# Choosing which waiting step an engine's queue takes next: a priority order in place of first ready, first served

## The chip, the cores and the metric

The kernel runs on one core of one Trainium2 chip. The metric is the device time of one execution in microseconds (us); less is better. Engines are called as in the profile: PE (TensorE, with PEld for its weight loads), DVE (VectorE), ACT (ScalarE), POOL (GpSimd) and SP (SyncE, which issues DMAs).

## What is computed

Three layers stand one behind the other:

```python
# 1. attention: 4 batches, 8 heads, 576 tokens, head size 64, window 128, ALiBi bias
scores = scale * q @ k.T + bias          # masked to 0 <= i-j < 128
x = softmax(scores) @ v                  # -> 2304 tokens x 512
# 2. dense feed-forward, 512 -> 2048 -> 512
g = softplus(x @ w_in); x = g @ w_out
# 3. noisy top-2 of 8 experts, 512 -> 1024 -> 512
noisy = x @ w_gate + softplus(x @ w_noise) * noise
out[t] = sum over the two best e of  softmax_e * relu(x[t] @ w1[e]) @ w2[e]
```

Layer 2's weights come as 64-bit floats, the rest as 32-bit. The kernel splits every matmul operand into a high and a low part and adds three products (high x high, high x low, low x high).

## The kernel before, in words

**The work.** The 2304 tokens are 9 chunks of 256. Layer 2 has 16 feed-forward blocks of 128; each needs a weight of `w_in` and one of `w_out`, so there are 32 weights, numbered w0 to w31 (even: `w_in`). A job is one block of one chunk: `mm1` (L542) multiplies up into a PSUM tile `h` and starts a softplus on ACT, DVE and POOL (L565 to L574); `mm2` (L583) multiplies down into `y` or `z` three jobs later. The jobs go first over blocks 0 to 5 of all chunks (54 jobs), while the attention of later chunks is woven in, then over blocks 6 to 15 chunk by chunk. Jobs 0 to 2 are blocks 0 to 2 of chunk 0; from job 3 on, chunk 1 and the rest of chunk 0 alternate, until block 5 of chunk 0 is job 9.

**Attention** goes by pieces: `step_a` (L327) has PE write scores, DVE add the bias with the row minimum (L350), ACT take exponentials (L356), DVE the reciprocal of the sums (L361, L362), and POOL (L370) or ACT (L368) normalise; `step_b` (L377) has PE transpose and DVE or ACT copy (L399, L397); `step_c` (L404) has PE multiply with `v`, then ACT and DVE evacuate the high and low part (L429, L434).

**Weight conversion** (`w_convert`, L476): SP loads 512 KB of raw doubles; ACT L486 and L490; DVE L494, L495 and L496, which are one step; POOL L512; ACT L500; DVE L504 (for every third weight from w12 on POOL); for some weights SP stores the result. Five are under way at once; the first 12 are due at the start, then one more every two jobs. **Weight splits** (`w2_split`, L1128) are layer 3's counterpart: ACT L1141 takes the high part of a loaded weight, DVE L1139 the low part.

**Expert phase.** Routing (L689 to L775) writes a table of tokens per expert; `late_table` (L951) plans groups of 256 tokens. `g_rows` (L1024) loads a group's rows by DMA and merges them on DVE (L1036, L1037); POOL gathers tokens (L1048); `s1`, `s2`, `s3` (L1175 to L1260) are the matmuls, with relu in L1187 and L1188 and results added to `out` by POOL (L1249).

**What sets the order.** PE's order is written out by hand. Every other engine gets its instructions in the order in which a planner, class `Order` (L26), lets them out while the program is built. A chain (L38) is a list of steps, each with an engine and an estimated cost (`ca`, `cv`, `cv2`, `cg`, L96 to L109). A heap holds each chain's next step at the time when it is ready. `_pop` (L48) takes the earliest step. Before, a step whose engine is busy is let out all the same and booked behind the engine's last one:

```python
if eng is not None:
    when = max(when, self.free.get(eng, 0.0))
```

So each queue is first ready, first served, with the older chain first only in a tie. `need` (L75) pops until a key is there, and moves PE's clock; `emitted` (L70) pops without moving it. On the chip an engine runs its queue in that order, whatever is ready.

Of the kernel before, what the change touches and what calls it, by code (L numbers as in the profile page):

```python
# [25 lines left out]
class Order:  # L26
# [8 lines left out]
        self.free = {}  # L35
        self.parked = {}

    def chain(self, *steps, after=0.0):  # L38

        heapq.heappush(self.heap, (self.now + after, self.count, steps, 0))  # L40
        self.count += 1

    def done(self, key, when):
# [2 lines left out]
            heapq.heappush(self.heap, (max(when, entry[0]),) + entry[1:])  # L46

    def _pop(self):  # L48
        entry = when, count, steps, i = heapq.heappop(self.heap)
        eng, cost, fn, key, needs = (tuple(steps[i]) + (None,) * 5)[:5]  # L50
        for n in needs or ():
            if n not in self.fin:
                self.parked.setdefault(n, []).append(entry)
                return
            if self.fin[n] > when:
                heapq.heappush(self.heap, (self.fin[n], count, steps, i))
                return
        if eng is not None:
            when = max(when, self.free.get(eng, 0.0))
        end = when + cost  # L60
        if eng is not None:
            self.free[eng] = end
        if fn is not None:
            fn()
        if key is not None:
            self.done(key, end)
        if i + 1 < len(steps):
            heapq.heappush(self.heap, (end + (0.1 if eng is not None else 0.0), count, steps, i + 1))

    def emitted(self, key):  # L70
        while key not in self.fin:
# [24 lines left out]
def ca(n):  # L96
    return 0.16 + n * 0.00083


def cv(n):  # L100
    return 0.15 + n * 0.00104
# [6 lines left out]
def cg(n):  # L108
    return 0.05 + n * 0.00275  # L109
# [3 lines left out]
def moe_chain_kernel(ctx, tc, qk, v, w_in, w_out, w_gate, w_noise, noise, w1, w2, out):  # L113
    nc = tc.nc
    PE, ACT, DVE, POOL, SP = nc.tensor, nc.scalar, nc.vector, nc.gpsimd, nc.sync
# [26 lines left out]

    o_ = Order()
    chain, spend, need, emitted, mark = o_.chain, o_.spend, o_.need, o_.emitted, o_.mark
    NDMA = 16

# [11 lines left out]
    def f32(ap):  # L158
        return ap.bitcast(F32)
# [3 lines left out]
    def tl(pool, shape, dtype, name, bufs, fin, tag=None, slots=None):  # L163

        r = rings.setdefault(name, [])
        while len(r) >= bufs:
            last = r[-bufs]
            (need if pool is psum else emitted)(last)
            if r[-bufs] == last:
                break  # L170
        r.append(fin)
        return pool.tile(shape, dtype, name=name, tag=tag or name, bufs=slots or bufs)
# [126 lines left out]
    def dma(fn, key=None, nbytes=1 << 18, after=0.0, needs=()):  # L299
        chain(("SP", 0.06, fn, None, needs), ("DMA", nbytes / 330e3, None), (None, 2.0, None, key), after=after)  # L300
# [26 lines left out]
    def step_a(m0):  # L327
# [16 lines left out]
        for x in range(2):  # L344
            s = tl(att, [P, 512], F32, "s", NS, ("be", m0 + x))
            s = s.rearrange("p (h t) -> p h t", h=2)
            M[m0 + x] = dict(s=s)
            for j in range(2):
                def tail(s=s, x=x, j=j):
                    DVE.tensor_tensor_reduce(s[:nq, j, :n], ps[j][:nq, x, :n],  # L350
                                             relh[:nq, 2 * (m0 % 4 + x) + j, r0:r0 + n],
                                             -(D ** -0.5), 3.0e38, OP.add, OP.min, st[:nq, 0, 2 * x + j:2 * x + j + 1])

                def ex(s=s, x=x, j=j):
                    y = slice(2 * x + j, 2 * x + j + 1)
                    ACT.activation(s[:nq, j, :n], s[:nq, j, :n], AF.Exp, bias=st[:nq, 0, y], scale=-1.0,  # L356
                                   accum_out=st[:nq, 1, y])
                chain(("V", cv(n), tail, ("ttr", m0 + x, j)), ("A", ca(n) + 0.2, ex, ("ex", m0 + x, j)))
# [112 lines left out]
    def w_tile():  # L471
        return wpool.tile([P, 2, 512], F32R, name="w", bufs=NRING)
# [3 lines left out]
    def w_convert(i):  # L476
        fc, half = divmod(i, 2)
        d = {}

        def load():  # L480
            raw = d["raw"] = wpool.tile([P, 512, 2], I32, name="raw", tag="w", bufs=NRING)
            SP.dma_start(raw.rearrange("p n z -> p (n z)"), (w_out if half else w_in).bitcast(I32)[fc])

        def first():
            d["a"] = tl(mid, [P, 512], I32, "cva", 4, ("wl", i))
            ACT.activation(f32(d["a"]), f32(d["raw"][:, :, 1]), AF.Abs)  # L486

        def third():
            lo32 = d["raw"][:, :, 0]
            ACT.activation(lo32, lo32.bitcast(U32), AF.Copy, scale=2.0 ** -29)  # L490

        def bits():
            a = d["a"]
            DVE.tensor_scalar(f32(a), f32(a), F64_LO, F64_HI, op0=OP.max, op1=OP.min)  # L494
            DVE.tensor_scalar(a, a, 3, 0x3FFFFFFF, op0=OP.logical_shift_left, op1=OP.bitwise_and)  # L495
            DVE.scalar_tensor_tensor(a, d["raw"][:, :, 1], -0x40000000, a, op0=OP.bitwise_and, op1=OP.bitwise_or)  # L496

        def high():
            W[i] = w_tile()
            ACT.activation(W[i][:, 0], f32(d["a"]), AF.Copy)  # L500

        def low():
            t = W[i]
            (DVE if (i < 2 * NA or LOWV[i % len(LOWV)]) else POOL).tensor_tensor(t[:, 1], f32(d["a"]), f32(t[:, 0]), OP.subtract)  # L504

        def store():
            if i in sidx:
                SP.dma_start(scratch[sidx.index(i)], f32(W.pop(i)).rearrange("p z n -> p (z n)"))
                nfreed[0] += 1
        chain(("SP", 0.06, load), ("DMA", (1 << 19) / 330e3, None), (None, 2.0, None),  # L510
              ("A", ca(512), first), ("A", ca(512), third), ("V", 2.2, bits),
              ("P", cg(512), lambda: POOL.tensor_tensor(d["a"], d["a"], d["raw"][:, :, 0], OP.add), ("wa", i)),  # L512
              ("A", ca(512), high),
              ("V", cv(512), low, ("wl", i)) if (i < 2 * NA or LOWV[i % len(LOWV)]) else ("P", cg(512), low, ("wl", i)),
              (None, 0.0, lambda: mark_now(("w", i), ("wl", i))),
              ("SP", 0.06, store, ("st", i)))

    def mark_now(key, of):
        o_.done(key, o_.fin[of])
# [279 lines left out]
    def convert_some():  # L799

        while nconv[0] < due[0] and live1() < room() and (nconv[0] < NCV or ("w", nconv[0] - NCV) in o_.fin):
            w_convert(nconv[0])
            nconv[0] += 1
# [281 lines left out]
    def ring_left():  # L1085
        return NRING - live1() - inring[0] - 2 * nsplit[0]
# [37 lines left out]
    def skip_singles():  # L1124
        while wsp[0] < wl[0] and groups[WJ[wsp[0]][0]][0] == 1:
            wsp[0] += 1

    def w2_split():  # L1128
        skip_singles()
        j = wsp[0]  # L1130
        if j >= wl[0] or not splitting[0] or nsplit[0] >= NSPLIT or nback[0] < len(sidx) or ring_left() < 2:
            return False
        wsp[0] += 1
        nsplit[0] += 1
        t = RAW2[j]
        hi, lo = W2[j] = [wpool.tile([P, 1024], F32R, name=x, tag="w", bufs=NRING) for x in ("whi", "wlo")]

        def low():
            DVE.tensor_sub(lo, t, f32(hi))  # L1139
            w2_drop(j)  # L1140
        chain(("A", ca(1024), lambda: ACT.activation(hi, t, AF.Copy), None, (("r2", j),)),  # L1141
              ("V", cv(1024), low, ("w2", j)))
        return True

    def w2_drop(j):
        del RAW2[j]
        if j in extra:
            extra.remove(j)
        else:
            inring[0] -= 1  # L1150

    def pump():
        while w2_load():
            pass
        while w2_split():
            while w2_load():
                pass
# [170 lines left out]
    for t in range(NT + max(L2, len(items) + 2)):  # L1328
# [11 lines left out]
        if t in starts:  # L1340
            c, n = starts[t]
# [110 lines left out]
```

## Time and profile before

| | |
|---|---|
| three runs, median (lowest to highest) | 1137.41 us (1136.45 to 1138.78) |
| the profiled execution's own time | 1136.42 us |
| its span, first to last instruction | 1134.2 us |
| PE busy in the span | 1071.8 us (94%) |
| DVE / ACT / POOL busy | 748.8 / 616.2 / 509.9 us (66 / 54 / 45%) |
| mean granted TensorE clock | 0.978 |

The busy shares are means over stages with different limits, so they are to be read stage by stage: where PE is idle or at a lower clock, and what ended its waits.

### The profile page before, as it was taken

Reading aid. Unit: us, or ns where it says so; the run is one execution under the profiler, and the core shown is the slowest. Engines: PE = TensorE matmul, PEld = TensorE weight load, DVE = VectorE, ACT = ScalarE, POOL = GpSimd, SP = SyncE. Lnnn points to the kernel's source line nnn. Section 1 sums busy time; section 2 is a strip of 40 time slices with the busy share of each in tenths; the row PEclk is TensorE's granted clock in tenths of the full one; section 3 lists DMA queues with packets and bytes.
Section 4 is the critical chain, followed back from the end, with each engine's and each line's share of the span. In section 5 each row is a group of like instructions: output and inputs, shape, how many; then the busy total and the mean of one; then the engine's idle time right before and its main releaser. Section 6 shows DMA issues by size and latency. Waiting matters only on the chain.

```text
span 1134.2 us, 20933 instructions
## 1 busy us (share of the span) xinstructions
PE 1071.8 (94%) x7021; PEld 914.2 (81%) x7021; DVE 748.8 (66%) x1946; ACT 616.2 (54%) x1459; POOL 509.9 (45%) x535
## 2 busy tenths in 40 slices
PE   5589999999999999999998997999999999999997
PEld 3477777777789888888887886997997997999984
DVE  8975799988885677777767685653653653655520
ACT  7876778877764444444444543553553553555531
POOL 3455677766675566666674232222122223222112
PEclk8699999999999999999999998999999999999999
DMA  8231544554683322112348829788887888888722
GB/s 306 102 94 57 181 161 141 202 206 146 199 318 121 121 76 75 52 62 76 96 153 304 251 28 339 206 233 263 227 233 259 232 227 254 250 225 233 215 56 38
DMA packets 96557, 198.90 MB, mean 175 GB/s; under 512 B 34049, under 2 KB 44801, under 8 KB 96449
## 3 DMA queue, kind: packets, MB, share of 16 engines
q1 hardware_dynamic: 86112, 176.01, 47.2%
q0 software_dynamic: 10336, 21.54, 9.6%
q8 instruction: 56, 0.92, 0.3%
q14 instruction: 53, 0.43, 0.1%
HBM read 157.82 MB, written 39.69 MB: 174 GB/s over the span
## 4 chain that ended last, share of the span: by engine, by line
PE 76%; DVE 11%; DMA 5%; ACT 3%; issue 2%; POOL 1%; SPq 1%; POOLq 0%; DVEq 0%; ACTq 0%
PE h L190 35%; PE y L190 24%; PE z L190 10%; PE t L201 4%; PE t L190 3%; PE t L339 2%; DMA raw<-in_moe_w_out 1%; DVE s L350 1%; ACT s L356 1%; DVE w L504 1%; DVE cva L495 1%; DMA rawp<-in_moe_w 1%; DVE cva L496 1%; DVE cva L494 1%; DVE su L573 1%
## 5 line engine op out<-in xcount | busy, mean ns | idle before, releaser
L190 PE MATMUL h<-xh,w 128*128 128x256 f32 x1152 | 238.8, 290 | 4.3 <-DVE sl L568 4.2
L1139 DVE TENSOR_TENSOR wlo<-rawp,whi 128x1024 fp32r<-128x1024 f32 x107 | 130.7, 1222 | 133.8 <-ACT whi L1141 127.4
L1249 POOL DMA_INDIRECT out<-ys,rc x41 | 83.3, 2031 | 272.3 <-DVE ys L1258 131.9
L190 PEld LDWEIGHTS h<-xh,w 128*128 128x128 f32 x1152 | 190.7, 193 | 18.2 <-DVE sl L568 9.3
L1141 ACT ACTIVATE whi<-rawp 128x1024 fp32r<-128x1024 f32 x107 | 113.4, 1060 | 149.1 <-PE h L190 98.0
L190 PE MATMUL y<-w,gh 128*128 128x512 f32 x552 | 179.3, 406 | 0.1
L190 PE MATMUL h<-xh,whi 128*128 128x256 f32 x576 | 165.5, 287 | 6.5 <-DVE gl L1188 6.5
L190 PE MATMUL h<-xl,w 128*128 128x256 f32 x576 | 164.2, 285 | 3.1 <-DVE xl L434 3.1
L574 POOL TENSOR_TENSOR su<-sa,su 128x256 f32<-128x256 f32 x144 | 112.6, 782 | 113.1 <-DVE su L573 98.3
L190 PE MATMUL h<-xl,whi 128*128 128x256 f32 x576 | 163.3, 284 | 0.0
L190 PE MATMUL h<-xh,wlo 128*128 128x256 f32 x576 | 163.3, 283 | 0.0
L565 ACT ACTIVATE sa<-h 128x256 f32<-128x256 f32 x144 | 54.8, 381 | 157.5 <-PE h L190 116.0
L190 PEld LDWEIGHTS h<-xh,whi 128*128 128x128 f32 x576 | 110.1, 191 | 14.1 <-DVE gl L1188 6.9
L569 POOL TENSOR_TENSOR sl<-sl,su 128x256 f32<-128x256 f32 x144 | 109.7, 762 | 17.3 <-DVE sl L568 5.8
L190 PEld LDWEIGHTS h<-xl,w 128*128 128x128 f32 x576 | 111.1, 193 | 6.4 <-DVE xl L434 3.5
L190 PEld LDWEIGHTS h<-xl,whi 128*128 128x128 f32 x576 | 110.2, 191 | 7.1 <-issue 1.4
L190 PEld LDWEIGHTS h<-xh,wlo 128*128 128x128 f32 x576 | 110.2, 191 | 0.0
L190 PEld LDWEIGHTS y<-w,gh 128*128 128x128 f32 x552 | 95.0, 191 | 16.9 <-issue 3.2
L190 PE MATMUL y<-w,gl 128*128 128x512 f32 x276 | 108.6, 393 | 0.0
L1048 POOL DMA_INDIRECT xg<-x1buf,rc x41 | 42.4, 1035 | 105.6 <-DVE rc L1037 60.4
L572 DVE TENSOR_TENSOR gl<-sl,gh 128x256 fp32r<-128x256 f32 x144 | 81.0, 563 | 9.4 <-ACT gh L570 6.6
L370 POOL TENSOR_TENSOR s<-s,st 128x512 f32<-128x512 f32 (+2 forms) x72 | 72.2, 1011 | 33.2 <-DVE st L362 19.4
(256 smaller groups left out, 2281.5 us busy)
## 6 DMA issues: line engine op xcount, KB each, us to landing
rawp<-in_moe_w SPq DMA_DIRECT2D x140, 512.0 KB
raw<-in_moe_w SPq DMA_DIRECT2D x44, 512.0 KB
qkT<-in_qk SPq DMA_DIRECT2D x20, 512.0 KB
raw<-in_moe_w_in SPq DMA_DIRECT2D x16, 512.0 KB
raw<-in_moe_w_out SPq DMA_DIRECT2D x16, 512.0 KB
out<-zero SPq DMA_DIRECT2D x19, 256.0 KB
xspill<-xh SPq DMA_DIRECT2D x9, 512.0 KB
xspill<-xl SPq DMA_DIRECT2D x9, 512.0 KB
```

Source lines behind the costliest of these rows:

```text
L190: PE.matmul(o, l, r, start=start, stop=stop)
L201: PE.transpose(o, i, idn)
L339: PE.matmul(ps[j][:nq, x, :n].rearrange("p (s t) -> p s t", t=P), qkT[hd, u % NQK, 0, hp, :nq], qkT[hd, sl, 1, hp, :], start=True, stop=True)
L370: POOL.tensor_tensor(s[:nq, :, :n], s[:nq, :, :n], st[:nq, 3, 2 * x:2 * x + 2, None].to_broadcast([nq, 2, n]), OP.mult)
L565: chain(("A", ca(CT), lambda: ACT.activation(a, ph, AF.Abs)), ("A", ca(CT), lambda: ACT.activation(a, a, AF.Exp, scale=-1.0), ("e", t)), ( ...
L569: ("P", cg(CT), lambda: POOL.tensor_add(l, l, u), None, (("d", t),)),
L572: ("V", cv(CT), lambda: DVE.tensor_sub(gl, l, f32(gh)), ("g", t)))
L574: ("P", cg(CT), lambda: POOL.tensor_tensor(u, a, u, OP.subtract), ("d", t)), after=2 * ca(CT) + 0.15)
L1048: POOL.indirect_dma_start(out=x, out_offset=None, in_=x1buf[:T - 3 * CT if g < NEARLY else TPAD, :], in_offset=bass.IndirectOffsetOnAxis(a ...
L1139: DVE.tensor_sub(lo, t, f32(hi))
L1141: chain(("A", ca(1024), lambda: ACT.activation(hi, t, AF.Copy), None, (("r2", j),)), ("V", cv(1024), low, ("w2", j)))
L1249: POOL.indirect_dma_start(out=out[:, :], out_offset=bass.IndirectOffsetOnAxis(ap=rc[:, a, 0:1], axis=0), in_=ys, in_offset=None, compute_o ...
```

## The change

A heap entry gets a rank, `later`, between its time and its chain's number. A step whose engine is busy is no longer booked: it goes back into the heap at the time when the engine comes free, and all the steps that wait there are compared by rank, then by age of chain. Weight conversions and weight splits get rank 1, all other chains 0.

```diff
-    def chain(self, *steps, after=0.0):
+    def chain(self, *steps, after=0.0, later=0):
-        heapq.heappush(self.heap, (self.now + after, self.count, steps, 0))
+        heapq.heappush(self.heap, (self.now + after, later, self.count, steps, 0))
...
-        entry = when, count, steps, i = heapq.heappop(self.heap)
+        entry = when, later, count, steps, i = heapq.heappop(self.heap)
...
-                heapq.heappush(self.heap, (self.fin[n], count, steps, i))
+                heapq.heappush(self.heap, (self.fin[n], later, count, steps, i))
                 return
-        if eng is not None:
-            when = max(when, self.free.get(eng, 0.0))
+        if eng is not None and self.free.get(eng, 0.0) > when:
+            heapq.heappush(self.heap, (self.free[eng], later, count, steps, i))
+            return
...
-            heapq.heappush(self.heap, (end + (0.1 if eng is not None else 0.0), count, steps, i + 1))
+            heapq.heappush(self.heap, (end + (0.1 if eng is not None else 0.0), later, count, steps, i + 1))
...  (w_convert)
-              ("SP", 0.06, store, ("st", i)))
+              ("SP", 0.06, store, ("st", i)), later=1)
...  (w2_split)
-              ("V", cv(1024), low, ("w2", j)))
+              ("V", cv(1024), low, ("w2", j)), later=1)
```

No instruction is added or taken away, no cost estimate changes, and PE's own order stays as it is written.

## Rows read from the trace of the kernel before

**Rows 1.** Busy time by stage: window, length, engines, PE clock, DMA share, GB/s.

```profile
18.00:45.00 27.00, 14.90 (x83) 11.10 (x83) 26.41 (x55) 21.28 (x56) 13.16 (x10) 0.62 0.29 114
45.00:72.00 27.00, 19.05 (x151) 14.28 (x152) 25.65 (x75) 22.79 (x66) 14.98 (x13) 0.87 0.34 116
72.00:116.00 44.00, 42.16 (x331) 34.25 (x330) 25.15 (x103) 28.59 (x99) 24.52 (x31) 1.00 0.27 82
116.00:350.00 234.00, 224.33 (x1658) 181.45 (x1657) 200.68 (x551) 172.78 (x519) 161.16 (x177) 0.99 0.57 196
350.00:600.00 250.00, 248.44 (x1639) 218.15 (x1637) 178.61 (x573) 115.57 (x298) 151.50 (x197) 1.00 0.28 90
600.00:700.00 100.00, 87.67 (x561) 78.14 (x560) 68.03 (x201) 43.38 (x79) 35.18 (x30) 0.96 0.71 229
```

**Rows 2.** Waits of PE, 0 to 75 us: us in total, times, longest.

```profile
PE y L201 <- POOL s L370: 12.1, 3, 5.8
PE t L201 <- POOL s L370: 6.1, 3, 3.4
```

**Rows 3.** Groups of DVE, 0 to 72 us, the conversions: busy us, mean ns.

```profile
L504 DVE TENSOR_TENSOR w<-cva,w 128x512 fp32r<-128x512 f32 x12 | 9.4, 789 | 0.0
L494 DVE TENSOR_SCALAR cva<-cva 128x512 f32<-128x512 f32 x12 | 8.7, 727 | 0.0
L496 DVE SCALAR_TENSOR_TENSOR cva<-raw,cva 128x512 int32<-128x512 int32 x12 | 8.3, 693 | 0.4
...
L495 DVE TENSOR_SCALAR cva<-cva 128x512 int32<-128x512 int32 x12 | 7.6, 630 | 0.4
```

**Rows 4.** Timelines of PE and DVE, 23 to 34 us: start, length.

```profile
23.86 2.08 PE L339 MATMUL h<-qkT 64*128 64x256 f32 x8
...
31.79 2.39 PE L339 MATMUL h<-qkT 64*128 64x256 f32 x8 [3.27 <-DVE st L350]
...
27.91 1.52 DVE L494 TENSOR_SCALAR cva<-cva 128x512 f32<-128x512 f32 x1
...
30.53 0.42 DVE L350 CUSTOM_DVE_ANT_0 s<-h,relh 128x256 f32<-128x256 f32 x1
```

**Rows 5.** Timelines of ACT, DVE and PE, 33 to 40 us.

```profile
33.41 0.18 ACT L356 ACTIVATION_READ_ACCUMULATOR s<-s,st 128x1 f32 x1
...
37.98 0.16 DVE L361 TENSOR_SCALAR st<-st 128x4 f32<-128x4 f32 x1
...
39.62 1.12 PE L201 MATMUL y<-ident,s 128*128 128x128 f32 x4 [4.39 <-POOL s L370]
```

**Rows 6.** Timelines of ACT and DVE, 594 to 600 us: weight splits.

```profile
594.61 3.89 ACT L1141 ACTIVATE whi<-raw 128x1024 fp32r<-128x1024 f32 x4
...
596.26 3.49 DVE L1139 TENSOR_TENSOR wlo<-raw,whi 128x1024 fp32r<-128x1024 f32 x3
```

**Rows 7.** Timeline of PE, 603 to 699 us: the waits.

```profile
603.60 0.39 PE L190 MATMUL h<-xh,w 128*128 128x256 f32 x1 [3.27 <-DVE sl L568]
...
652.63 0.18 PE L190 MATMUL t<-mcum,ones 128*128 128x8 bf16 x1 [1.97 <-DVE mcum L757]
...
698.75 0.58 PE L190 MATMUL h<-xh,whi 128*128 128x256 f32 x1 [6.49 <-DVE gl L1188]
```

**Rows 8.** Groups of ACT and POOL, 0 to 72 us, the conversions: busy us, mean ns.

```profile
L490 ACT ACTIVATE raw<-raw 128x512 int32<-128x512 uint32 x12 | 8.0, 665 | 0.0
L486 ACT ACTIVATE cva<-raw 128x512 f32<-128x512 f32 x12 | 7.9, 658 | 0.6 <-DVE w L504 0.6
...
L500 ACT ACTIVATE w<-cva 128x512 fp32r<-128x512 f32 x12 | 7.5, 622 | 0.7 <-POOL cva L512 0.7
...
L512 POOL TENSOR_TENSOR cva<-cva,raw 128x512 int32<-128x512 int32 x12 | 16.7, 1390 | 26.0 <-DVE cva L496 16.6 <-DVE su L573 2.2 <-ACT pT L397 1.6
```

**Rows 9.** Timeline of DVE before the last of these waits.

```profile
696.42 0.17 DVE L1036 TENSOR_REDUCE rc<-rk 128x2 int32<-128x8 int32 x1 [9.23 <-DMA rk<-rect]
```

**Rows 10.** Instructions of L494, 0 to 72 us: ns min/median/max, starts.

```profile
L494 DVE TENSOR_SCALAR cva<-cva x12: 396/422/1524, 14.6 to 59.3; 128x512 f32<-128x512 f32 x12
```

## The prediction, made before the changed kernel ran

> **What bounds the kernel now.** I read the stages first, since only a stage in which PE idles has anything for a new order to give [rows 1]. From 350 to 600 us PE is busy 248.4 of 250 us. Before that it idles: 12.1 us of the 27 from 18 to 45, 8.0 of the 27 from 45 to 72, 1.8 of the 44 from 72 to 116, 9.7 of the 234 from 116 to 350; and after it 12.3 of the 100 from 600 to 700. In the first two of these DVE is busy 26.4 and 25.7 of 27 us: DVE is the bound there. PE's waits come next. Most of the start's idle time is waits for normalised scores from POOL, 12.1 and 6.1 us [rows 2]; POOL itself is busy only half the time, so what is late stands upstream. The groups of DVE then show with what it is filled: the twelve weight conversions take 9.4 + 8.7 + 8.3 + 7.6 = 34.0 us, 2.84 us each [rows 3]. The timelines show them standing ahead of attention. PE had written scores at 23.86 + 2.08 = 25.94 us; DVE began a further conversion at 27.91 and took up the scores at 30.53, and PE waited 3.27 us [rows 4]. Again: the exponentials were complete at 33.59 us, the sums' step (L361) ran at 37.98, and PE waited 4.39 us [rows 5].
>
> From 594.6 us ACT ran four weight splits back to back, 3.9 us, and DVE three of their low parts, 3.5 us; the softplus of a running job stood behind them, and PE waited 3.27 us [rows 6, 7].
>
> **The change, part by part.** Nothing is added; every term is a wait that goes or comes.
>
> *Start, 0 to 72 us.* The waits at stake are 12.1 + 6.1 + 3.3 = 21.5 us [rows 2, 4]. Of the two followed above, the first goes whole: at 27.91 us the ready scores would have been taken before a rank-1 step. The second goes too, since the sums' chain is older than what ran before it and the rest were conversions. That is 3.3 + 4.4 = 7.7 us. Of the other 13.8 I take half, 6.9: a conversion that has begun isn't broken off, and its three DVE operations are one step, 0.73 + 0.63 + 0.69 = 2.05 us [rows 3]; and part of any such wait is the latency of DVE, ACT and POOL in a row, which stays. Gain 14.6 us; bounds 0 (the planner's times are so far off that the same steps meet) and 21.5.
>
> The work put off doesn't vanish. 14.6 us of DVE are the work of 14.6 / 2.84 = 5 conversions, which move past 72 us. They are w6 and up, first needed from job 4 on. From 72 to 116 us DVE idles 44 - 25.15 = 18.9 us [rows 1], so they fit, but tightly, and PE will meet some weights that aren't ready. I give back a third, 4.9 us; bounds 0 and 14.6. Net of the start: 9.7 us. The granted clock is 0.62 from 18 to 45 us [rows 1], so part of PE's work there runs at the lower of its two levels; that a denser PE gets some of this back I leave at nothing, since the waits stay many.
>
> *Other queues.* POOL's part of a conversion, 1.39 us [rows 8], now goes behind a waiting normalisation: part of the waits above. On SP the loads of raw weights go behind attention loads and spills that wait at that moment, and a sixth conversion's load is let out only after the first is done. I price this at nothing, because five conversions lie ahead of any late one; if that cover goes, a transfer that is late costs what the nearest row of one does, up to 9.2 us [rows 9]. ACT's three parts (0.67 + 0.66 + 0.62 us) [rows 8] go behind exponentials; ACT idles 5.7 and 4.2 us in the two stages [rows 1], so they find room.
>
> *116 to 350 us.* Twenty more conversions, DVE busy 200.7 of 234 us. PE idles 9.7 us [rows 1]. The same collisions are rarer; I take 2 us, bounds 9.7 gained and 9.7 lost (a weight late at the jobs of block 6 and up). From 350 to 600 us PE has 1.6 us to give: nothing.
>
> *Splits at 594.6 us.* The softplus now goes first; a split already running still holds DVE for 3.49 / 3 = 1.16 us, on average half of it. 3.3 - 0.6 = 2.7 us gained, bounds 3.3 and -3.5 (the expert phase's first weight late by the three low parts moved).
>
> *Waits at 652.6 and 698.8 us,* 1.97 and 6.49 us [rows 7]. The first stands behind a split, but the table's chains leave a gap between two steps, in which a waiting split gets in before as after. The second has DVE's queue blocked for 9.23 us by a merge that waits for a DMA [rows 9]; the change doesn't see real DMA times. I take 0 for both, bounds 8.5 either way. After 700 us, with PE full as from 350 to 600 us, I take nothing.
>
> **Sum.** -9.7 - 2.0 - 2.7 = -14.4 us. Against the profiled execution's 1136.42 us: 1122.0. The median of the runs lies 1.0 above that execution, so the forecast is 1123.0 us.
>
> **The rivals.**
>
> *Put-off conversions collide with POOL: 1130 us.* From 72 to 116 us POOL is busy 24.5 of 44 us [rows 1], and L494, 0.42 us in the median, took up to 1.52 [rows 10]. If L494 and L495 of all five put-off conversions were 1.1 us longer, DVE would need 14.6 + 5 x 2 x 1.1 = 25.6 us where 18.9 are idle; PE would stand for the 6.7 missing, and the sum would be -7.7: 1129.7. The Trainium skill, SBUF — State Buffer, section "Who interferes with whom", says that DVE's two-port operations and POOL share one pair of ports, and that whichever starts second is blocked until the first has finished; by that rule such collisions are whole instructions, not a slow-down, and the case gets the more weight. The trace agrees at its maximum and not at its median: over twelve the mean is 727 ns [rows 3]. For it: conversions now run where POOL has softplus work; against: the start has as much POOL work. Chance 0.16.
>
> *Little changes: 1137 us.* If in the planner's times two steps seldom wait for one engine at once, or one of each pair stays a 2 us conversion in progress, queues come out nearly as before. Against it: 4.4 us of conversions and others in one place [rows 5]. Chance 0.09.
>
> *Weights too late: slower.* Lowest rank knows no due date: a weight that PE wants next waits behind attention that only later chunks want. The place is mm1 and mm2 of chunk 0's blocks 3 to 5, w6 to w11. The price of a weight on which PE finds nothing begun is the whole row of steps: 0.66 + 0.67 + 2.05 + 1.39 + 0.62 + 0.79 = 6.2 us [rows 3, 8]. Against the gains without the give-back, 14.6 + 2.0 + 2.7 = 19.3 us, it decides from the fourth exposed weight on (3.1 x 6.2 = 19.3). With five exposed: 31.0 - 19.3 = +11.7, 1149 us. Against it: five conversions are under way at once and the older goes first among them, so they overlap, and DVE's idle time after 72 us is about as long as the work put off. Chance 0.13.
>
> **How the numbers follow.** The forecast has 0.62. Faster: 0.62 + 0.16 = 0.78; the same: 0.09; slower: 0.13 (within 0.2%, 2.3 us, a measurement of this kernel can't tell it from no change). The range reaches down to the start's whole 21.5, 3.3 of the splits and half of the 9.7: 29.7 below the median, 1107.7, set at 1107; and up over the second rival to the edge of "the same", 1139.5. Left out: the slower case, and little below.
>
> **What would show it.** Right: the waits for POOL L370 in the first 75 us fall from 18.2 us to under 10; PE becomes dense (busy over 95%) at about 60 us in place of 72; conversions on DVE last until some 90 to 110 us in place of 67; the wait at 603.6 us is under 1 us, with splits spread among the softplus steps. The give-back shows as waits of PE for DVE w L504 between 60 and 110 us, 5 us in all. Wrong: such waits over 15 us; or the waits for L370 stay at 18; or new waits of PE between 116 and 350 us over 10 us; or the 6.49 us at 698.8 us grow or vanish, which would move the sum by a term that I put at 0.

## The result, and the profile after

The changed kernel is slower: 1147.68 us in the median of 5 runs (1144.71 to 1148.68) against 1136.45 us (1135.94 to 1138.78) for the kernel before on the same chip, a ratio of 1.0086 with a 95% interval of 1.0068 to 1.0104 (ratios, here and below, are not quotients of medians; that would be 1.0099). The forecast was 1123.0 us, in a range of 1107 to 1139.5. The profiled execution took 1145.68 us, 2.0 below the median, and its span is 1143.9 us, 9.8 more than before. All lines of the code lie 2 further down, and 4 in the experiments in ready order (10 behind the edit of e11). A matmul carries the line of the helper that issues it (L190 before, L192 here), a transpose likewise (L201, L203).

First the stages of the changed kernel, as in [rows 1]: window, length, busy time of PE, PEld, DVE, ACT and POOL, granted PE clock, DMA share, GB/s.

```profile
18.00:45.00 27.00, 19.79 (x133) 14.18 (x134) 23.78 (x73) 24.05 (x68) 12.03 (x11) 0.77 0.33 122
45.00:72.00 27.00, 23.68 (x193) 18.64 (x192) 24.38 (x73) 23.23 (x71) 16.68 (x18) 0.91 0.62 195
72.00:116.00 44.00, 36.68 (x251) 29.17 (x250) 32.44 (x98) 27.18 (x87) 24.73 (x29) 0.92 0.16 55
116.00:350.00 234.00, 215.08 (x1583) 172.56 (x1582) 202.02 (x535) 167.18 (x504) 154.37 (x168) 0.97 0.53 185
350.00:600.00 250.00, 246.40 (x1614) 215.79 (x1614) 170.74 (x571) 111.97 (x292) 149.62 (x197) 1.00 0.26 85
600.00:700.00 100.00, 92.96 (x595) 82.29 (x594) 69.15 (x202) 47.14 (x88) 37.08 (x35) 0.97 0.68 212
```

The first two rows are the gain: PE idles 7.2 and 3.3 us there, 10.5 in all against 20.1 before. The third and fourth are the loss: 7.3 us against 1.8, and 18.9 against 9.7, both at a lower clock than before.

PE's order is the same in both kernels, so progress can be read job by job. The table gives the start of a job's first mm1 matmul in the profiled executions; for the changed kernel and all experiments below it is the difference to before, in us. Layer 2 has jobs 0 to 143; 148, 164 and 172 count on into the expert phase, where `s1` fills the tile `h` by twelve matmuls as mm1 does: they are its 5th, 21st and 29th filling.

| kernel | job 2 | job 9 | job 40 | job 56 | job 148 | job 164 | job 172 | span |
|---|---|---|---|---|---|---|---|---|
| before (time) | 71.3 | 103.1 | 272.8 | 335.8 | 626.0 | 677.6 | 709.6 | 1134.2 |
| after | -12.7 | -2.0 | +9.1 | +10.3 | +12.7 | +15.8 | +10.0 | +9.8 |
| e1_defer | +0.5 | +0.5 | +1.3 | +2.5 | +2.9 | +4.4 | +4.5 | +4.5 |
| e2_age | +17.7 | +19.2 | +31.4 | +31.9 | +34.7 | +35.1 | +27.7 | +27.7 |
| e3_ready_rank | -14.0 | +0.8 | +0.2 | -0.7 | -1.1 | -3.3 | -2.9 | -3.3 |
| e4_due | -3.5 | +4.3 | +14.8 | +15.6 | +18.5 | +18.9 | +14.1 | +14.0 |
| e5_age_copies | -12.4 | +0.7 | +2.3 | +3.6 | +6.0 | +9.2 | +4.5 | +4.5 |
| e6_ready_conv | -13.9 | +1.0 | +0.3 | -0.6 | -1.2 | +0.3 | +0.1 | +0.2 |
| e7_ready_pool | -13.7 | +5.7 | +6.5 | +5.6 | +5.2 | +3.8 | +3.5 | +3.5 |
| e8_ready_due | -7.9 | +4.1 | +5.1 | +4.2 | +3.7 | +3.3 | +4.2 | +4.2 |
| e9_loads_early | +12.0 | +12.0 | +14.0 | +15.1 | +13.0 | +10.9 | +11.9 | +11.8 |
| e10_ready_copies | -10.1 | +7.8 | +9.1 | +9.2 | +9.8 | +8.4 | +8.6 | +8.4 |
| e11_three_steps | -7.5 | +8.0 | +7.3 | +8.4 | +8.4 | +8.3 | +8.5 | +8.3 |
| e12_mixed | -13.5 | +1.2 | +4.2 | +3.4 | +1.4 | -0.7 | +0.4 | +0.1 |

The second row is the whole story of the change: 12.7 us won by job 2, 10.7 of them lost again by job 9, 12.3 more lost from job 9 to job 56, and 0.5 won from there to the end: -12.7 + 10.7 + 12.3 - 0.5 = +9.8. (One profiled execution is not the median: those of e1, e5, e7, e10 and e12 lie 1.4 to 4.2 us above their kernels' medians. Verdicts below go by the ratios; the table says where time goes.)

**Won: the start.** PE's waits in the changed kernel, 0 to 75 us: us in total, times, longest.

```profile
PE y L203 <- POOL s L372: 6.1, 3, 2.3
PE t L203 <- POOL s L372: 2.4, 2, 2.1
```

They answer to [rows 2]: 18.2 us became 8.5. The conversions' groups of DVE, 0 to 110 us, show that their work is the same and only later; the last of the twelve ends at 96.2 us, not 67.4:

```profile
L498 DVE SCALAR_TENSOR_TENSOR cva<-raw,cva 128x512 int32<-128x512 int32 x12 | 9.3, 777 | 0.4
L506 DVE TENSOR_TENSOR w<-cva,w 128x512 fp32r<-128x512 f32 x12 | 9.0, 765 | 0.0
L496 DVE TENSOR_SCALAR cva<-cva 128x512 f32<-128x512 f32 x12 | 7.9, 659 | 0.1
...
L497 DVE TENSOR_SCALAR cva<-cva 128x512 int32<-128x512 int32 x12 | 7.6, 631 | 0.4
```

**Lost: jobs 2 to 9.** Between the start of job 2 and that of job 9 PE has the same 239 matmuls to do. The stretch in the kernel before, then in the changed one:

```profile
71.30:103.10 31.80, 30.50 (x239) 24.68 (x237) 18.98 (x80) 21.42 (x77) 18.80 (x24) 1.00 0.37 112
```

```profile
58.60:101.10 42.50, 34.76 (x239) 27.57 (x237) 37.64 (x102) 28.51 (x89) 28.31 (x30) 0.90 0.33 96
```

The 10.7 us lost are 6.4 of idle time (7.7 against 1.3) and 4.3 of longer matmuls (34.76 - 30.50) at a granted clock of 0.90 in place of 1.00. The timeline of PE names the wait, and the windows around it the clock:

```profile
66.56 0.51 PE L192 MATMUL h<-xh,w 128*128 128x256 f32 x2 [0.95 <-DVE w L506]
...
81.61 0.79 PE L192 MATMUL h<-xh,w 128*128 128x256 f32 x2 [4.30 <-DVE w L506]
```

```profile
77.00:81.60 4.60, 0.30 (x2) 0.10 (x1) 4.57 (x15) 4.46 (x14) 3.30 (x5) 0.89 0.58 214
81.60:85.00 3.40, 3.39 (x14) 3.30 (x15) 3.33 (x6) 1.05 (x4) 2.22 (x2) 0.50 0.00 0
85.00:90.00 5.00, 5.00 (x31) 3.76 (x32) 4.14 (x9) 1.30 (x4) 2.76 (x3) 0.76 0.01 3
```

PE waits 4.30 us for one put-off weight while DVE is full, and comes back at half the clock, the lower of its two levels, for at least 3.4 us. So this wait is paid twice.

**Lost: 116 to 350 us.** From job 13 to job 40 PE does 1098 matmuls. Before, then after:

```profile
122.50:272.80 150.30, 143.40 (x1098) 113.29 (x1096) 136.90 (x393) 116.55 (x365) 105.19 (x114) 0.98 0.49 173
```

```profile
121.70:281.90 160.20, 146.56 (x1098) 115.34 (x1096) 139.31 (x391) 116.12 (x365) 103.15 (x112) 0.96 0.44 155
```

9.9 us lost: 6.7 idle, 3.2 at a lower clock. The largest of PE's waits in 116 to 350 us has a new name, the copies of step_b (L399); before, the same line had 0.7 us in one wait:

```profile
PE t L192 <- ACT pT L399: 7.5, 5, 4.2
```

The longest of the five, in the timeline of PE, and what ACT ran ahead of that copy:

```profile
173.95 0.69 PE L192 MATMUL t<-pT,rawv 128*64 128x128 f32 x4 [4.19 <-ACT pT L399]
```

```profile
170.43 0.66 ACT L488 ACTIVATE cva<-raw 128x512 f32<-128x512 f32 x1 [4.24 <-DMA raw<-in_moe_w_in]
171.00 0.49 ACT L358 ACTIVATE s<-s,st 128x256 f32<-128x256 f32 x1
...
172.78 0.49 ACT L358 ACTIVATE s<-s,st 128x256 f32<-128x256 f32 x1
...
173.53 0.36 ACT L399 ACTIVATE pT<-t 128x256 f32<-128x256 f32 x1
```

PE stood from 169.76. ACT's queue was blocked until 170.43 by a conversion whose raw data were not there; then came that conversion and four exponentials of scores that PE had written ahead, and only then, at 173.53, the copy for which PE stood. The exponentials belong to the older chain, so age puts them first; the copy is the younger and the more urgent. The kernel before has such a stall as well, and there the copy follows close behind it and PE waits 0.68 us:

```profile
168.45 0.67 ACT L486 ACTIVATE cva<-raw 128x512 f32<-128x512 f32 x1 [3.55 <-DMA raw<-in_moe_w_in]
...
169.29 0.37 ACT L397 ACTIVATE pT<-t 128x256 f32<-128x256 f32 x1
```

Late raw data alone are not the cause of this stage's loss: from 116 to 350 us ACT waits 5.6 us for them here and 4.2 before, but 3.8 in e1, which loses 0.8 us from job 9 to 40, and 1.4 in e2, which loses 12.2.

**The transition.** PE's waits of the changed kernel, 540 to 720 us:

```profile
PE t L192 <- DVE mcum L759: 3.3, 2, 2.4
PE t L192 <- DVE r_mb L706: 3.2, 1, 3.2
PE y L192 <- DVE x L644: 2.7, 2, 1.6
PE h L192 <- DVE gl L1190: 2.2, 1, 2.2
```

Of [rows 7] the 3.27 us at 603.6 are gone and the 6.49 at 698.8 are 2.2; L706 (0.6 us before, as L704) and L644 are new. By stretches of the same jobs the changed kernel loses 2.9 us from job 56 to 141 (both waits for L644 lie there), gains 0.5 from 141 to 148, where the wait for L706 has taken the place of the one at 603.6, loses 3.0 from 148 to 164, gains 5.7 from 164 to 172 (the wait at 698.8: 4.2 us less idle, and 1.6 us because PE then stays at the higher clock, 1.00 in place of 0.89), and 0.3 from there on. The loss up to 141 and the gain at 698.8 are age's: in the four kernels with age (this one, e2, e4, e5) PE idles 3.6 us from job 56 to 141 and 0.9 to 2.3 from 164 to 172, in the nine experiments in ready order 1.4 to 1.8 and 6.1 to 7.2.

### The profile page after: what moved, and what is told of

Read it like the earlier page. It is cut to its first block, busy times and chain, and to the rows that moved or that the text cites. A ratio compares the mean times of both kernels' runs of the same rounds, so it can differ in the third digit from the quotient of the medians.

```text
span 1143.9 us, 20825 instructions
## 1 busy us (share of the span) xinstructions
PE 1078.4 (94%) x7021; PEld 916.4 (80%) x7021; DVE 757.1 (66%) x1946; ACT 613.6 (54%) x1459; POOL 504.4 (44%) x535
## 4 chain that ended last, share of the span: by engine, by line
PE 73%; DVE 12%; ACT 5%; DMA 3%; POOL 2%; issue 2%; SPq 0%; POOLq 0%; DVEq 0%; ACTq 0%
PE h L192 34%; PE y L192 22%; PE z L192 9%; PE t L203 4%; PE t L192 3%; DVE su L575 2%; ACT s L358 2%; PE t L341 1%; DVE s L352 1%; DVE gl L574 1%; DVE sl L570 1%; DVE cva L497 1%; DVE cva L498 1%; DVE cva L496 1%; POOL sl L571 1%
## 5 line engine op out<-in xcount | busy, mean ns | idle before, releaser
L192 PE MATMUL h<-xh,w 128*128 128x256 f32 x1152 | 240.5, 291 | 7.5 <-DVE w L506 5.3
L1251 POOL DMA_INDIRECT out<-ys,rc x41 | 80.4, 1960 | 292.4 <-DVE ys L1260 131.0
L192 PEld LDWEIGHTS h<-xh,w 128*128 128x128 f32 x1152 | 191.6, 194 | 21.6 <-DVE w L506 5.7
L192 PE MATMUL y<-w,gh 128*128 128x512 f32 x552 | 178.9, 405 | 2.7 <-DVE x L644 2.7
L1189 ACT ACTIVATE gh<-h 128x256 fp32r<-128x256 f32 x144 | 55.3, 384 | 221.2 <-PE h L192 202.1
L192 PE MATMUL h<-xh,whi 128*128 128x256 f32 x576 | 166.0, 288 | 2.3 <-DVE gl L1190 2.2
L192 PE MATMUL h<-xl,w 128*128 128x256 f32 x576 | 164.6, 286 | 1.1 <-DVE xl L436 1.1
L192 PE MATMUL h<-xl,whi 128*128 128x256 f32 x576 | 163.7, 284 | 0.5 <-DVE xl L1069 0.5
L192 PE MATMUL h<-xh,wlo 128*128 128x256 f32 x576 | 163.6, 284 | 0.0
L576 POOL TENSOR_TENSOR su<-sa,su 128x256 f32<-128x256 f32 x144 | 109.4, 760 | 98.5 <-DVE su L575 76.9
L1190 DVE SCALAR_TENSOR_TENSOR gl<-h,gh 128x256 fp32r<-128x256 f32 x144 | 60.5, 420 | 137.0 <-ACT gh L1189 128.0
L571 POOL TENSOR_TENSOR sl<-sl,su 128x256 f32<-128x256 f32 x144 | 112.4, 780 | 24.9 <-DVE rec L706 5.6
L192 PEld LDWEIGHTS h<-xh,whi 128*128 128x128 f32 x576 | 110.7, 192 | 10.4 <-DVE gl L1190 3.2
L192 PEld LDWEIGHTS h<-xl,whi 128*128 128x128 f32 x576 | 110.7, 192 | 7.7 <-issue 1.4
L192 PEld LDWEIGHTS h<-xl,w 128*128 128x128 f32 x576 | 111.7, 194 | 4.6 <-DVE xl L436 1.5
L192 PEld LDWEIGHTS h<-xh,wlo 128*128 128x128 f32 x576 | 110.6, 192 | 0.0
L192 PEld LDWEIGHTS y<-w,gh 128*128 128x128 f32 x552 | 94.2, 190 | 20.2 <-DVE x L644 4.6
L192 PE MATMUL y<-w,gl 128*128 128x512 f32 x276 | 108.3, 392 | 0.0
```

Source lines behind the costliest of these rows:

```text
L192: PE.matmul(o, l, r, start=start, stop=stop)
L571: ("P", cg(CT), lambda: POOL.tensor_add(l, l, u), None, (("d", t),)),
L576: ("P", cg(CT), lambda: POOL.tensor_tensor(u, a, u, OP.subtract), ("d", t)), after=2 * ca(CT) + 0.15)
L1189: chain(("A", ca(CT), lambda: ACT.activation(gh, ph, AF.Relu)), ("V", cv(CT), lambda: DVE.scalar_tensor_tensor(gl, ph, 0.0, f32(gh), op0=O ...
L1190: ("V", cv(CT), lambda: DVE.scalar_tensor_tensor(gl, ph, 0.0, f32(gh), op0=OP.max, op1=OP.subtract), ("hr2", g, f)))
L1251: POOL.indirect_dma_start(out=out[:, :], out_offset=bass.IndirectOffsetOnAxis(ap=rc[:, a, 0:1], axis=0), in_=ys, in_offset=None, compute_o ...
```

## The experiments

The change has three parts: a step whose engine is busy is deferred (*deferral*); among waiting steps the older chain goes first (*age*); conversions and splits have rank 1 (*rank*). The main tool is the kernel with another tie-break, called ready order below: each entry keeps the time at which its step became ready, and that is compared in place of age.

```diff
...
-            heapq.heappush(self.heap, (self.free[eng], later, count, steps, i))
+            heapq.heappush(self.heap, (self.free[eng], later, ready, count, steps, i))
...  (`ready` is carried along in every entry)
```

### e1_defer: deferral alone

Ready order, and no chain has a rank.

```diff
-              ("SP", 0.06, store, ("st", i)), later=1)
+              ("SP", 0.06, store, ("st", i)))
...
-              ("V", cv(1024), low, ("w2", j)), later=1)
+              ("V", cv(1024), low, ("w2", j)))
```

> Deferral alone: a step of a busy engine goes back into the heap, but those that wait are compared by the time at which they were ready, and conversions and splits have rank 0 like the rest. Three theories. Rank (conversions put last make weights late): nothing of it is here, so 1136 us, within 3 us of the kernel before. Age (older chain first puts young but urgent steps behind old ones): nothing of it here either, 1136 us. Deferral itself (steps are let out later against PE's own order): the whole loss is here, about 1148 us.

Measured: 1138.55 us, ratio 1.0005 (0.9991 to 1.0019). Deferral by itself does nothing that can be measured, and leaves the start as it was (+0.5 at jobs 2 and 9).

### e2_age: deferral and age, no rank

The changed kernel with the two `later=1` taken out, as above, and age kept.

> Deferral and age, as in the changed kernel, but conversions and splits have rank 0. Age theory: no gain at the start, and the 14.6 us that the changed kernel lost between the 14th and the 38th job are here, so about 1151 us. Rank theory: about 1136 us, since no conversion is put last. Both in parts: between 1140 and 1146 us.

Measured: 1163.32 us, ratio 1.0235 (1.0218 to 1.0252). Two waits in the timeline of PE make the start's loss:

```profile
29.70 0.69 PE L203 MATMUL y<-ident,s 128*128 128x128 f32 x2 [16.45 <-POOL s L372]
...
54.89 1.11 PE L203 MATMUL y<-ident,s 128*128 128x128 f32 x4 [17.51 <-POOL s L372]
```

The conversions that begin with the kernel are the oldest chains; by age they go ahead of all attention. The time is 12 us above what the age theory had, since the start itself loses 17.7 by job 2. With no rank involved, jobs 9 to 40 still lose 12.2 us (+19.2 to +31.4), about as many as the changed kernel's 11.1 (-2.0 to +9.1). So the loss after 116 us is age's, not the rank's. The steps that it hits are not the same as there, though: from 116 to 350 us PE waits 10.5 us here for the low part of step_c (DVE, L436; 2.4 before) and only 0.8 for the copies in L399.

### e3_ready_rank: deferral and rank, ready order

The changed kernel with the tie-break above.

> Deferral and rank, but steps of one rank are compared by the time at which they were ready, not by the age of their chain. Age theory: the gain at the start (some 12 us) and what is given back to late weights (some 9 us) stay, and the 14.6 us lost between the 14th and the 38th job are gone: about 1133 us. Rank theory: that loss stays, about 1147 us.

Measured: 1133.26 us, ratio 0.9967 (0.9954 to 0.9981): faster than both kernels. By the ratios 1.2% separate it from the changed kernel, and the tie-break is the only difference. The start's gain is there (-14.0 at job 2) and is given back whole by job 9 (+0.8), then nothing is lost up to job 56. The give-back in the timeline of PE, and in the stretch of the same matmuls:

```profile
68.16 0.80 PE L194 MATMUL h<-xh,w 128*128 128x256 f32 x2 [4.35 <-DVE w L508]
84.72 0.51 PE L194 MATMUL h<-xh,w 128*128 128x256 f32 x2 [2.72 <-DVE w L508]
...
97.55 0.50 PE L194 MATMUL h<-xh,w 128*128 128x256 f32 x2 [1.54 <-DVE w L508]
```

```profile
57.30:103.90 46.60, 36.18 (x238) 28.29 (x237) 41.71 (x108) 30.02 (x94) 29.50 (x30) 0.89 0.33 99
```

Of 14.8 us, 9.1 are idle time (10.4 against 1.3; 8.6 of it these three waits) and 5.7 are the clock (36.18 against 30.50).

### e4_due: weights of the first jobs without rank

The changed kernel (age), with w6 to w11 at rank 0.

```diff
-              ("SP", 0.06, store, ("st", i)), later=1)
+              ("SP", 0.06, store, ("st", i)), later=int(i < 6 or i >= 2 * NA))
```

> The changed kernel, but the conversions of w6 to w11, which PE wants soonest after the start, have rank 0; the others keep rank 1. Late weights as read in the trace (PE waits 4.3 us for a conversion's last step at 81.6 us, then runs at the lower clock; 8.7 us lost between the 6th and the 8th job): that stretch's loss goes, about 1139 us if the start keeps its gain, and about 1145 if the six conversions take the gain of the start with them. If that stretch's loss has another cause: 1147 us.

Measured: 1149.92 us, ratio 1.0117 (1.01 to 1.0134), above all three expected times. Job 2 gains only 3.5 us: at rank 0 and by age these chains again go ahead of attention. One wait of 9.5 us shows it, in PE's waits from 0 to 75 us:

```profile
PE t L203 <- POOL s L372: 9.7, 2, 9.5
```

### e5_age_copies: the copies of step_b first

The changed kernel, with rank -1 for the copies for which PE waited.

```diff
-            chain(ev + (("b", m, x),))
+            chain(ev + (("b", m, x),), later=-1)
```

> The changed kernel with one exception to age: the copies of transposed scores (step_b), which are young chains on whose result PE's next attention piece waits, get a rank ahead of all others. If age costs its 14 us between the 14th and the 38th job because these copies stand behind the exponentials of an older chain (PE waits 10.0 us for ACT's copies in the changed kernel, 0.7 before), the waits for them fall under 2 us and the time to 1138 to 1141 us. If age does its harm elsewhere (softplus steps of the newest job behind older attention), about 1147 us.

Measured: 1137.94 us, ratio 1.0008 (0.9983 to 1.0033), and no wait for L399 is left between 116 and 350 us. The stretch from job 13 to job 40, the same matmuls but one:

```profile
124.00:275.10 151.10, 142.28 (x1097) 112.74 (x1095) 136.20 (x388) 116.91 (x362) 103.34 (x111) 0.99 0.46 163
```

151.1 us where the changed kernel needs 160.2 and the kernel before 150.3: one kind of step, let past older exponentials, brings back 9.1 of the 9.9 us. What keeps e5 behind e3, 7.8 us in the two profiles (4.7 by the ratios), lies about half before job 56 (+3.6 against -0.7) and half behind it: up to job 164 e5 loses 5.6 us where e3 gains 2.6, and up to job 172 it wins 4.7 back. That second part is age again: e10 below has the same edit in ready order, and goes from +9.2 to +8.4 between jobs 56 and 164. The waits for L644 (2.7 us, none in e10) are one piece of it; the rest wasn't tried.

### e6_ready_conv: splits without rank

e3, with the splits back at rank 0.

```diff
-              ("V", cv(1024), low, ("w2", j)), later=1)
+              ("V", cv(1024), low, ("w2", j)))
```

> Deferral and rank in order of readiness, but rank 1 for conversions alone; splits have rank 0. If the splits' rank is what gains around 600 us: the 3.3 us wait of PE there is back, and the time some 2 to 3 us above that of deferral and rank together, 1135.5 us. If splits matter nothing: 1133 us.

Measured: 1136.43 us, ratio 0.9991 (0.9978 to 1.0003). Up to job 141 it goes as e3, to 0.2 us. Then the wait of [rows 7] is back, in the timeline of PE:

```profile
603.01 0.39 PE L194 MATMUL h<-xh,w 128*128 128x256 f32 x1 [3.25 <-DVE sl L572]
```

e3 has 0.2 us there and begins job 143 4.8 us earlier than e6. At job 148 both stand alike again (-1.1 and -1.2), because in e3 PE then runs into the routing's own steps on DVE:

```profile
612.84 0.18 PE L194 MATMUL t<-r_mb,tri 128*128 128x8 bf16 x1 [2.63 <-DVE r_mb L708]
```

So this wait is moved, not removed: from job 141 to 148 PE idles 3.2 us in e6 and 3.4 in e3. The two profiles part after that, from job 148 to 164; before, e6, e3:

```profile
626.00:677.60 51.60, 49.63 (x330) 44.35 (x329) 37.86 (x109) 26.95 (x46) 15.08 (x10) 1.00 0.51 140
624.80:677.90 53.10, 51.13 (x330) 45.63 (x329) 38.14 (x109) 26.92 (x46) 16.57 (x10) 0.97 0.47 137
624.90:674.30 49.40, 49.40 (x329) 44.35 (x328) 37.15 (x107) 26.64 (x46) 15.79 (x10) 1.00 0.52 145
```

The wait of 1.97 us for `mcum` [rows 7] stands in the first two and is gone in e3; e6 pays 1.5 us for it by the clock on top, which the kernel before, with the same wait, doesn't. By the ratios the rank of the splits is worth 0.0024 of 1137 us, 2.7 us (0.6 to 4.8 by the two intervals), of e3's whole 3.8; what is left with the conversions' rank alone can't be told from nothing.

### e7_ready_pool: the conversions' last step on POOL

e3, with the low part (L508) of w6 to w11 on POOL in place of DVE.

```diff
-            (DVE if (i < 2 * NA or LOWV[i % len(LOWV)]) else POOL).tensor_tensor(
+            (DVE if (i < NA or i >= 2 * NA and LOWV[i % len(LOWV)]) else POOL).tensor_tensor(
```

> Deferral and rank in order of readiness, and the last step of w6 to w11 (6 x 0.79 us of DVE) on POOL, 1.35 us each. If the gain of the start is given back because DVE's work until the 9th job is conserved: 4.7 us less DVE work there, so up to 4.7 us less, 1129 us. If it is given back because lowest rank starts those conversions too late, with DVE idle in between: no gain, since the chain of one conversion grows by 0.6 us, 1133 to 1135 us.

Measured: 1136.68 us, ratio 0.998 (0.997 to 0.999), a little above both expected times, with job 9 at +5.7. Six steps less on DVE (6 x 0.79 us by [rows 3]) don't make the weights earlier; PE's waits, 45 to 103 us, have only changed their name:

```profile
PE h L194 <- POOL w L508: 7.6, 3, 3.5
...
PE h L194 <- ACT w L504: 2.3, 1, 2.3
```

### e8_ready_due: e4's edit in ready order

> Deferral and rank in order of readiness, with rank 0 for w6 to w11, so that they compete by readiness as before. If late starts are the cause: the three waits of PE for a conversion's last step (8.6 us in deferral and rank together) fall under 3 us while most of the 14 us at the second job stay, 1127 to 1129 us. If DVE's work is conserved: what is saved there is lost before the second job, 1133 us.

Measured: 1139.4 us, ratio 1.0005 (0.999 to 1.002), above both expected times. PE's waits for these weights fall from 8.6 to 2.0 us, and what that saves is paid before: job 2 gains 7.9 us in place of 14.0, and job 9 stands at +4.1.

### e9_loads_early: raw data there early

e3, with the loads of raw weights as chains of their own at rank 0, and up to eight conversions under way in place of five.

```diff
-        chain(("SP", 0.06, load), ("DMA", (1 << 19) / 330e3, None), (None, 2.0, None),
-              ("A", ca(512), first), ("A", ca(512), third), ("V", 2.2, bits),
+        chain(("SP", 0.06, load), ("DMA", (1 << 19) / 330e3, None), (None, 2.0, None, ("ld", i)))
+        chain(("A", ca(512), first, None, (("ld", i),)), ("A", ca(512), third), ("V", 2.2, bits),
...
-        while nconv[0] < due[0] and live1() < room() and (nconv[0] < NCV or ("w", nconv[0] - NCV) in o_.fin):
+        while nconv[0] < due[0] and live1() < room() and (nconv[0] < 8 or ("w", nconv[0] - 8) in o_.fin):
```

> The ready-order kernel with ranks (e3), and the raw loads of conversions as chains of their own with rank 0, up to eight under way in place of five; the conversions' other steps keep rank 1. Theory A (the start's gain is given back because put-off conversions begin late: in e3 the seventh raw load was issued at 36.4 us): with the loads there early, PE's waits for DVE w fall from 8.6 us to under 4, job 9 stands at -4 or better against before (e3 +0.8), time about 1129. Theory B (the twelve conversions' work on DVE and behind it has to be done before job 9 whatever the order): job 9 at 0 to +2, PE's waits for DVE w still 6 to 9 us, time 1132 to 1135.

Measured: 1148.44 us, ratio 1.0102 (1.0086 to 1.0117). Of theory A the first half came: the twelfth weight was done at 72.4 us (99.5 in e3), and PE waited for none. Its time did not, and neither did theory B's. PE stood still elsewhere: 9.9 us for a copy of step_b (L401) before 45 us, and then, in the timelines of PE and ACT:

```profile
61.23 0.58 PE L194 MATMUL h<-xh,w 128*128 128x256 f32 x1 [14.46 <-ACT xh L433]
```

```profile
49.16 0.63 ACT L504 ACTIVATE w<-cva 128x512 fp32r<-128x512 f32 x1 [2.23 <-POOL cva L516]
50.77 0.67 ACT L490 ACTIVATE cva<-raw 128x512 f32<-128x512 f32 x1 [0.98 <-DVE w L508]
...
60.23 0.67 ACT L490 ACTIVATE cva<-raw 128x512 f32<-128x512 f32 x1 [0.98 <-DVE w L508]
60.81 0.37 ACT L433 ACTIVATE xh<-t 128x256 fp32r<-128x256 f32 x1
```

The tile `cva` has four buffers. With more than four conversions begun, taking a fifth buffer makes the planner let out the steps that will free one, whatever waits (`tl`, through `emitted`), and on the chip ACT's queue then holds conversion steps that wait for POOL and DVE ahead of the copy (L433) that PE needs. So the run doesn't answer what early raw data alone would do. A fifth buffer wasn't tried.

### e10_ready_copies: e5's edit in ready order

> The ready-order kernel with ranks (e3), and the copies of step_b with rank -1. Theory (the copies' place in ACT's queue costs PE only where age puts them behind exponentials; in ready order they already stand right): within 2 us of e3's 1133.3, PE's waits for ACT pT at 1 us or less as in e3. Rival (young urgent copies wait behind ready exponentials in every order): the stretch from 116 to 350 us gains 3 to 5 us and the time is about 1129.

Measured: 1140.16 us, ratio 1.001 (0.9998 to 1.0023), its runs spread from 1137.58 to 1144.38, and the profile caught the longest. Both expectations miss the time. From job 9 to job 56 the kernel loses 1.4 us where e3 gains 1.5, so copies had nothing to win there in ready order, against the rival. In this longest run 7 us lie before job 9 (+7.8 against +0.8), for the most part in a stage that in e3 has a clock of 0.93:

```profile
72.00:116.00 44.00, 37.30 (x228) 29.30 (x228) 32.67 (x87) 25.89 (x79) 23.39 (x27) 0.81 0.16 49
```

PE was as busy as e3's (37.39 us there) and got through 228 matmuls in place of 257. By the ratios a usual run is 4.9 us behind e3; where it loses them isn't shown, since the runs differ in the clock (mean 0.974 in the longest, 0.982 in the shortest).

### e11_three_steps: a conversion that can be interrupted

e3, with the three DVE operations L494 to L496 as steps of their own.

```diff
-              ("A", ca(512), first), ("A", ca(512), third), ("V", 2.2, bits),
+              ("A", ca(512), first), ("A", ca(512), third), ("V", 0.74, bits), ("V", 0.73, bits2), ("V", 0.73, bits3),
```

> The ready-order kernel with ranks (e3), with the conversion's three DVE operations (L494 to L496 of the kernel before) as three steps in place of one, so that an attention step waits for 0.7 us of a conversion at most and not for 2.05. Theory (a conversion that has begun isn't broken off, and that is part of what is left of the start's waits): PE's waits for POOL s in the first 75 us fall by 1 to 3 us from e3's, and are given back by job 9 like the rest: time 1131 to 1134. Rival (what is left is the latency of DVE, ACT and POOL in a row): no change at the start, 1133, or 1 to 3 us worse since conversions are later still.

Measured: 1144.81 us, ratio 1.0061 (1.0047 to 1.0076), worse than both expectations. The waits for POOL in the first 75 us stay (9.0 us against 9.5 in e3), so breaking the conversion up doesn't shorten them. The weights come later still; PE's waits, 0 to 103 us:

```profile
PE h L194 <- ACT w L510: 9.1, 3, 6.1
...
PE h L194 <- DVE w L514: 5.6, 3, 2.6
```

### e12_mixed: age among conversions only

e3, with conversions and splits compared by age, all others by ready time.

```diff
-            heapq.heappush(self.heap, (self.free[eng], later, ready, count, steps, i))
+            heapq.heappush(self.heap, (self.free[eng], later, 0.0 if later else ready, count, steps, i))
```

> The ready-order kernel with ranks (e3), with age of chain kept for rank 1 alone: waiting attention, softplus and other steps are compared by the time at which they became ready, waiting conversions and splits by age. Theory (late weights are late partly because in ready order five conversions advance side by side and none is finished early; the older first finishes w6 sooner): PE's waits for DVE w fall from e3's 8.6 us to about the changed kernel's 5.3, job 9 stands at -3 to -1 against before (e3 +0.8), the steady stage stays at 0 as in e3, time 1129 to 1132, the fastest of all. Rival (the start is bound by what DVE and ACT have to do before job 9): as e3, 1133, job 9 at 0 to +1.

Measured: 1134.58 us, ratio 0.9972 (0.9959 to 0.9984), e3's equal: the rival's time. PE's waits for weights fall, as the theory had it, from 8.6 to 6.3 us (45 to 103 us), and job 9 stands at +1.2 all the same, because in this execution the 238 matmuls run at a clock of 0.85:

```profile
PE h L194 <- DVE w L508: 6.3, 3, 2.7
```

```profile
57.80:104.30 46.50, 37.26 (x238) 29.08 (x237) 41.35 (x107) 29.86 (x93) 29.45 (x30) 0.85 0.30 88
```

## Why the prediction was wrong, step by step

From forecast to result the spans are 24.2 us apart (-14.4 against +9.8): 7.7 of them arise up to job 9, 14.3 from there to job 56, 2.2 behind it.

**The start's gain: right.** 14.6 us were forecast; job 2 came 12.7 us earlier, of which 11.3 are idle time and 1.4 shorter matmuls at a higher clock. The waits for L370 fell to 8.5 us (under 10 was the mark), PE was dense from 58 us on (7.60 of 8 us up to 66), though not after 77, and the conversions ended at 96.2 (90 to 110).

**The give-back: mis-sized.** The step "I give back a third, 4.9 us" measured 10.7 in the changed kernel, and the whole 14.8 in e3. It went by DVE's idle time from 72 to 116 us, where the work put off would fit; but weights have due times, and from 77 to 81.6 us, where PE needed one, DVE was busy 4.57 of 4.6 us. The waits themselves were close to the forecast 5 us (5.3). What the sum left out is that PE comes back from them at the lower clock: 4.3 of the 10.7 us. "I leave at nothing" was said of a gain by the clock; against the 1.4 us gained up to job 2 stands this loss. e7, e8, e9, e11 and e12 each moved or shortened one part of this work, and in none of them was job 9 earlier than in e3; by age it was, in the changed kernel (-2.0). That the start is bound by the conversions and attention together, in whatever order, is what the five suggest; no run proves that a better order doesn't exist.

**116 to 350 us: the step that failed.** "The same collisions are rarer; I take 2 us" gained, with 9.7 lost as the far bound; the loss from job 9 to job 56 was 12.3. Only the rank was costed there. The other half of the new rule, that among steps of equal rank the older chain goes first, was used as an argument for the gain at [rows 5] and priced at nothing elsewhere. e2 shows the loss without any rank, e3 shows it gone with the tie-break changed, and e5 shows which steps carry it in the changed kernel: the young copies of step_b behind older exponentials on ACT (in e2 it is others, the low parts of step_c). The question that the prediction asked of waiting conversions, who is queued behind and who waits for that, was not asked of attention's own steps. The sign named for it, new waits of over 10 us, wasn't reached: PE's idle time grew by 9.2 us there, and the rest of the loss is the clock.

**The splits: the number by another path.** Forecast 2.7 us, and e3 against e6 gives 2.7 by the ratios, but that they agree is luck. The wait at 603.6 us, from which the 2.7 were worked out, went as forecast (3.25 us in e6, 0.2 in e3), and PE paid it back at the routing's steps before job 148. What e3 keeps comes from the wait at 652.6 us, which the prediction put at 0. The one at 698.8 us, put at 0 too and named as a sign, is no better in e3 (7.1 us); in the changed kernel age shortened it to 2.2, worth 5.7 us, and lost nearly as much elsewhere behind job 56: in all 0.5 us gained there in place of 2.7.

**The rivals.** Collisions with POOL: the twelve conversions took 9.3 + 9.0 + 7.9 + 7.6 = 33.8 us of DVE against 34.0 before, so moving them cost nothing there. Weights too late: its time, 1149, is near the measured 1147.7, but not its mechanism. It had five exposed weights and 31 us at the start; two waits of 5.3 us in all came, and the slower end came from age.

## What to carry to other kernels

A priority rule has a tie-break, and with few ranks the tie-break decides most of the order: cost it like the ranks, and look for a young chain on which the bound engine waits next. Here ready time was the safe one, and age lost 1.2%, though at one place, the wait at 698.8 us, age was the better. Work that is put off at a start bound by several engines is owed by its due time, not by the end of the stage; look at idle time just before the due time. A wait that goes is won only as far as the next one: follow PE past it. And a wait of PE is to be costed with the clock after it, by comparing stretches with the same matmuls.

## What was not expected of the hardware

The size of the clock's part. After one wait of 4.30 us the granted clock of the next 3.4 us is 0.50, where the kernel before has 1.00 in the same stretch, and over jobs 2 to 9 the same matmuls take 30.50 us before, 34.76 after, 36.18 in e3 and 37.26 in e12. e12 has fewer waits for weights than e3 and pays as much. Nor is the price fixed: behind the same wait of 1.97 us for `mcum` the clock stayed at 1.00 in the kernel before and fell in e1 and e6 (0.97 over the stretch, 51.13 us for 330 matmuls against 49.63). And it differs from run to run of one program: e5 took 1133.03 us at a mean clock of 0.986 and 1145.41 at 0.972, so the shares of the clock read from one profiled execution are that execution's. The Trainium skill, TensorE: Matmul & The Clock Gate, section "HAM oscillation — how this bites in real kernels", describes a PE that waits for data between bursts of matmuls and starts each burst at the lower clock; the trace agrees with its 0.50 behind the wait of 4.30 us.
